# A new start order for a gated FFT and MLP mixer: dummy matmuls, block-wise hand-over, reordered vector work

## The chip, the cores and the metric

The kernel runs on one core of a Trainium2 chip. The metric is device time in microseconds (us) of that core for one launch. A run is called fast or slow by its state: slow means over 1.5% above the fastest run of the same kernel. Engines are called by their names in the profile: PE is the matmul engine, DVE the vector engine, ACT the scalar engine (activation functions, scaled copies), POOL the third elementwise engine, SP the engine whose queue issues most loads.

## The reference

Two branches read the same input x of S = 2048 rows and D = 512 columns and are mixed by a gate per row.

```python
x = A_x                                             # (1, 2048, 512) bf16
g = sigmoid((x * gate_w).sum(-1, keepdims=True))
# branch A: spectral mixing
a = irfft2(rfft2(x) * (w_r + 1j * w_i), s=(S, D))
# branch B: token MLP, along the rows; F = 1792
h = layernorm(x, axis=-1)
u = gelu(einsum("bsd,sf->bdf", h, w1) + b1)
b = (einsum("bdf,fs->bds", u, w2) + b2).transpose(0, 2, 1)
return g * a + (1 - g) * b
```

## The kernel before

Branch B is two matmul layers. The first one (`u`) has 14 groups of 16 matmuls; six groups use weights `w1a` and are accumulated side by side in six PSUM banks while the 16 row blocks of x come in, eight groups use weights `w1b` later. The second layer (`yb`) is 16 groups of 14 matmuls.

Branch A is a chain: DVE folds the transposed input into `xf`; PE does the transform along D (matmuls `f<-tf,xf`, called f1 below); ACT copies the result to `xdt`; DVE does a 16-point FFT (`pa` ... `fu`); PE does a second transform stage (`f<-fu,tce`, called f3); DVE multiplies by the spectral weights; then the way back: matmuls `i`, a second FFT on DVE (ending in `zt`), matmuls `ya`. PE fills its time between the steps of A with matmuls of B, in an order fixed when the kernel is built. In the first part the other engines are given their instructions in the order in which they are written. In the trace DVE keeps this order up to `xf`; the few instructions that stand behind `xf` in that part run mixed among those of the FFT.

The parts that the change touches (cuts marked):

```python
for b0, b1 in ((0, 2), (2, 6), (6, 11), (11, 16)):       # loads: x and its weights in turn
    w = wts.tile([P, b1 - b0, FT1 * P], BF16, tag="wt", name="w1a")
    nc.sync.dma_start(out=x[:, b0:b1], in_=xv[:, b0:b1])
    nc.sync.dma_start(out=w[:], in_=w1v[:, b0:b1, 0:FT1 * P])
# ... cut: bias loads; then xt (transposed x) and w1b loads; iotas in F32; tables tf
moments(0, 1)                       # mean and variance on DVE, 1/sqrt on POOL
# ... cut: index work for the tables
normal(0, 1, on_act=False)          # hn = (x - mean) * rstd, then six matmuls per block
moments(1, 3)
moments(3, 6)
normal(1, 3, on_act=False)
normal(3, 6)                        # from here on ACT writes hn
# ... cut: groups of three and four blocks, index work (fill_marg, tg) in between
nc.vector.tensor_add(marg3[:, 0], ea[:], m0[:, None, :].to_broadcast([P, NE, P]))
# ... cut: more index work, then prod = x * gate_w, then last of all:
for h in range(2):
    hs = slice(h * H, (h + 1) * H)
    nc.vector.tensor_add(xf[:, 0, :, hs], xt[:, 0:2, hs], xt[:, 2:4, hs])
    nc.vector.tensor_sub(xf[:, 1, :, hs], xt[:, 0:2, hs], xt[:, 2:4, hs])
# ... cut: gelus of the six groups, f1 with its copies, sine tables, gate sums
pw = a_bank("l0w")                  # a small reordering matmul, ahead of the FFT in the text
nc.tensor.matmul(pw[:, 0:64], lhsT=pmB[:], rhs=ws[:].rearrange("p e c w -> p (e c w)"),
                 start=True, stop=True)
# ... cut: arithmetic on its result
fft16(nc, tmp, xdt[:], fa[:], fu[:], inverse=False)
for e in range(NE):
    bank = a_bank("f3")
    nc.tensor.matmul(bank[:], lhsT=tce[:, 1, e, :], rhs=fu[:, e].rearrange("p c l -> p (c l)"),
                     start=True, stop=False)
    # ... cut
```

## Time and profile before

| | before |
|---|---|
| median of the first 4 runs (lowest to highest) | 156.96 us (156.03 to 157.4) |
| median of all 16 runs beside the result | 156.91 us (155.55 to 158.39) |
| span of the profiled run | 154.9 us |
| PE busy by the page | 136.2 us |
| PE work counted by matmul pitch | 124.7 us |

The pitch count is explained in the prediction below. It is needed since the recorded length of a matmul is not the time it takes from its neighbours: matmuls of 512 columns are recorded with a mean of 379 ns here, but follow each other every 216 ns. The Trainium skill, "Perfetto Trace Analysis", section "Tensor Engine Instruction (MATMUL, LD_WEIGHTS)", says that the end of a matmul is estimated by the profiler and is "a model, not a measurement"; this trace agrees.

From the page of the kernel before: the span, the busy times (us, share of the span, number of instructions), and the shares of engines in the chain of work that ended last.

```profile
span 154.9 us, 2013 instructions
...
PE 136.2 (88%) x697; PEld 68.1 (44%) x697; DVE 116.5 (75%) x279; ACT 94.7 (61%) x150; POOL 12.8 (8%) x37
...
DVE 58%; PE 21%; ACT 11%; issue 3%; DMA 3%; POOL 2%; POOLq 0%; ACTq 0%; DVEq 0%
```

The PE timeline of the kernel before from its start to the first matmuls with `w1b` (columns: start in us, length in us, engine, line, operation, out<-in, shapes, how many in a row, and in brackets the idle time before and what ended it):

```profile
6.85 0.18 PE L296 MATMUL bias_t<-ident,bias_rows 30*128 30x30 bf16 x1 [6.85 <-DVE ident L270]
7.34 2.72 PE L248 MATMUL u<-hn,w1a 128*128 128x512 bf16 x6 [0.31 <-DVE hn L245]
11.47 22.04 PE L248 MATMUL u<-hn,w1a 128*128 128x512 bf16 x90 [1.41 <-DVE hn L245]
34.55 1.67 PE L492 MATMUL u<-hn,w1b 128*128 128x512 bf16 x7 [1.03 <-ACT gl L334]
```

The first six matmuls take 2.72 us, about twice what six of them take later. As in the prediction, "first layer" means from here on the six groups with `w1a` alone, and "second-layer" matmuls those with `w1b`. The first layer begins at 7.34 us, and the first matmul with `w1b` stands at 34.55 us. This last number, "the start of `w1b`", is the mark for how long the first layer took.

All waits of PE in the kernel before (what waits, for what, us in total, times, longest):

```profile
PE bias_t L296 <- DVE ident L270: 6.8, 1, 6.8
PE l0w L379 <- DVE ws L377: 1.7, 1, 1.7
PE u L248 <- DVE hn L245: 1.7, 2, 1.4
PE ya L478 <- DVE zt L98: 1.2, 1, 1.2
PE ya L478 <- ACT eo L481: 1.1, 1, 1.1
PE u L492 <- ACT gl L334: 1.0, 1, 1.0
PE f L343 <- DVE xf L328: 0.3, 1, 0.3
```

The DVE timeline of the kernel before, around `xf` (same columns):

```profile
37.39 1.22 DVE L328 TENSOR_TENSOR xf<-xt 128x2048 bf16<-128x2048 bf16 x1
...
40.79 1.22 DVE L329 TENSOR_TENSOR xf<-xt 128x2048 bf16<-128x2048 bf16 x1
50.88 1.22 DVE L39 TENSOR_TENSOR pa<-xdt 128x2048 bf16<-128x2048 bf16 x1 [8.88 <-ACT xdt L345]
```

In the list of waits, the first line is only the start; the others are what the change may win. The last piece of `xf` ends at 42.0 us, 9 us after the last transposed input landed (32.94 us), and the FFT starts at 50.88 us.

The place of the wait for the small matmul, from the DVE and the PE timeline of the kernel before:

```profile
73.53 1.22 DVE L98 TENSOR_TENSOR fu<-pb,qb 128x2048 bf16<-128x2048 bf16 x1
78.45 0.41 PE L379 MATMUL l0w<-ws,pmB 128*128 128x64 f32 x2 [1.73 <-DVE ws L377]
```

The first piece of `fu` was ready at 74.75 us, 2 us before PE began to wait (76.72 us). f3 itself could have started then; only the small matmul, which stood ahead of it, could not.

One wait of this list is an accident of the profiled run, as its DVE timeline shows:

```profile
135.28 0.43 DVE L511 TENSOR_TENSOR ot<-tbv,ap 128x512 bf16<-128x512 bf16 x1 [1.27 <-DMA out_dram<-ot]
```

Here the second store of the output landed 3.89 us after its issue, while it takes 1.79 us in the profile of before_warm (below), which has the same instructions in this stage. The wait of 1.1 us for `eo` followed from it. So about 1.4 us of the profiled span of the kernel before are not there to be won by the change.

### The profile page before, as it was taken

To read this page: it belongs to the slowest core of one execution; us is meant where nothing else is said; L and a number is where in the kernel's file an instruction comes from. 1 tells how busy PE (TensorE), PEld (TensorE's weight loads), DVE (VectorE), ACT (ScalarE), POOL (GpSimd) and SP (SyncE) were. 2 spreads that over 40 slices of the span, in tenths; PEclk is the share of its full clock that TensorE was granted. 3 is DMA by queue.
4 is the path that set the end of the run, shared out by engine and by line. 5 is a ranking of instruction groups with operands and counts; after the bars stand their busy time and mean duration, and the time that the engine had idled before them with its cause. 6 is when DMAs were issued, how large, how long until landed. Compare 5 with 4: busy or idle time off the path is not lost.

```text
span 154.9 us, 2013 instructions
## 1 busy us (share of the span) xinstructions
PE 136.2 (88%) x697; PEld 68.1 (44%) x697; DVE 116.5 (75%) x279; ACT 94.7 (61%) x150; POOL 12.8 (8%) x37
## 2 busy tenths in 40 slices
PE   0169999979999999999879999999999969969990
PEld 0023444433555544444345564465444435645430
DVE  3998979969800499999986999508999999598111
ACT  3305764997199999999529895475232244778221
POOL 7127625000000000000000000000000000000000
PEclk9999999999999999999999999999999999999997
DMA  4999999999999006180700700430348000424210
GB/s 145 353 383 389 244 205 297 200 280 347 340 292 320 15 0 181 56 235 14 225 0 28 213 2 0 129 108 4 99 138 236 1 0 0 140 102 142 92 37 34
DMA packets 41816, 23.33 MB, mean 151 GB/s; under 512 B 9008, under 2 KB 41776, under 8 KB 41808
## 3 DMA queue, kind: packets, MB, share of 16 engines
q1 hardware_dynamic: 41696, 23.08, 52.1%
q0 software_dynamic: 112, 0.14, 0.4%
q8 instruction: 5, 0.08, 0.2%
q14 instruction: 3, 0.02, 0.1%
HBM read 19.02 MB, written 2.10 MB: 136 GB/s over the span
## 4 chain that ended last, share of the span: by engine, by line
DVE 58%; PE 21%; ACT 11%; issue 3%; DMA 3%; POOL 2%; POOLq 0%; ACTq 0%; DVEq 0%
PE yb L505 9%; DVE stats L230 6%; PE f L343 5%; DVE ta L407 3%; DVE tb L408 3%; DMA out_dram<-ot 3%; ACT tice L204 2%; DVE prod L323 2%; ACT tce L204 2%; ACT hn L242 2%; DVE marg L258 2%; DVE y L409 2%; PE ya L478 2%; DVE pb L39 2%; POOL rstd L234 2%
## 5 line engine op out<-in xcount | busy, mean ns | idle before, releaser
L505 PE MATMUL yb<-gl,w2t 128*128 128x512 bf16 x224 | 53.6, 379 | 0.0
L505 PEld LDWEIGHTS <-w2t 128*128 128x128 bf16 x224 | 21.9, 98 | 21.4 <-issue 0.2
L492 PE MATMUL u<-hn,w1b 128*128 128x512 bf16 x128 | 29.3, 379 | 1.0 <-ACT gl L334 1.0
L507 ACT ACTIVATE tbv<-yb,ombb,omg 128x512 bf16<-128x512 f32 x16 | 12.4, 777 | 23.8 <-PE yb L505 22.4
L248 PE MATMUL u<-hn,w1a 128*128 128x512 bf16 x96 | 24.8, 425 | 1.7 <-DVE hn L245 1.7
L492 PEld LDWEIGHTS <-w1b 128*128 128x128 bf16 x128 | 12.5, 98 | 14.9 <-issue 1.3
L248 PEld LDWEIGHTS <-w1a 128*128 128x128 bf16 x96 | 10.2, 106 | 16.0 <-issue 7.1
L242 ACT ACTIVATE hn<-x,nmr,rstd 128x512 bf16<-128x512 bf16 x13 | 9.6, 802 | 9.2 <-DVE nmr L239 7.1
L481 ACT ACTIVATE eo<-ya,gs 128x512 bf16<-128x512 f32 x16 | 10.5, 687 | 5.6 <-DVE ap L484 3.5
L511 DVE TENSOR_TENSOR ot<-tbv,ap 128x512 bf16<-128x512 bf16 x16 | 6.6, 420 | 8.8 <-ACT tbv L507 7.5
L345 ACT CAST xdt<-f 128x512 bf16<-128x512 f32 x16 | 10.7, 734 | 3.7 <-DVE xf L329 3.2
L418 ACT CAST xs<-f 128x512 bf16<-128x512 f32 x16 | 9.1, 587 | 4.1 <-PE f L417 3.8
L478 PE MATMUL ya<-tg,zt 128*128 128x256 bf16 x64 | 9.3, 271 | 2.5 <-DVE zt L98 1.2
L466 ACT CAST vp<-i 128x512 bf16<-128x512 f32 x16 | 8.8, 586 | 2.8 <-PE i L464 2.6
L352 ACT ACTIVATE junk<-prod 128x512 bf16<-128x512 bf16 x16 | 10.0, 626 | 0.3
L230 DVE BATCH_NORM_STATS2 stats<-x 128x6 f32<-128x512 bf16 x16 | 10.1, 680 | 0.0
L343 PE MATMUL f<-tf,xf 128*128 128x256 bf16 x64 | 9.6, 271 | 0.4 <-DVE xf L328 0.3
L334 ACT ACTIVATE gl<-u,biases 128x512 bf16<-128x512 f32 x14 | 9.0, 684 | 0.8 <-PE u L492 0.8
L478 PEld LDWEIGHTS <-zt 128*128 128x128 bf16 x64 | 6.1, 97 | 6.7 <-issue 2.7
L343 PEld LDWEIGHTS <-xf 128*128 128x128 bf16 x64 | 6.0, 96 | 5.2 <-issue 3.2
L462 PE MATMUL i<-tice,y 128*128 128x256 bf16 x32 | 7.8, 272 | 0.1
L39 DVE TENSOR_TENSOR pa<-xdt 128x2048 bf16<-128x2048 bf16 x1 | 1.2, 1224 | 8.9 <-ACT xdt L345 8.9
(178 smaller groups left out, 182.7 us busy)
## 6 DMA issues: line engine op xcount, KB each, us to landing
w2t<-in_B_w_dram SPq DMA_DIRECT2D x8, 896.0 KB, 4.9
w1b<-in_B_w_dram SPq DMA_DIRECT2D x4, 1024.0 KB, 7.2
out_dram<-ot SPq DMA_DIRECT2D x16, 128.0 KB, 1.7
w1a<-in_B_w_dram SPq DMA_DIRECT2D x2, 960.0 KB, 10.7
x<-in_A_x_dram SPq DMA_DIRECT2D x2, 640.0 KB, 9.6
wri<-in_A_w_r_dram SPq DMA_DIRECT2D x1, 1028.0 KB, 9.6
wri<-in_A_w_i_dram SPq DMA_DIRECT2D x1, 1028.0 KB, 10.2
w1a<-in_B_w_dram SPq DMA_DIRECT2D x1, 768.0 KB, 6.9
```

The source lines that it names most:

```text
L230: nc.vector.bn_stats(out=stats[:, b, :], in_=x[:, b, :])
L242: nc.scalar.activation(hn[:, b, :], x[:, b, :], ActF.Identity, bias=nmr[:, b:b + 1], scale=rstd[:, b:b + 1])
L248: nc.tensor.matmul(u1[ft][:], lhsT=w1a[b][:, ft * P:(ft + 1) * P], rhs=hn[:, b, :], start=(b == 0), stop=(b == NB - 1))
L343: nc.tensor.matmul(bank[:, par * L:(par + 1) * L], lhsT=xf[:, par, kt, b * P:(b + 1) * P], rhs=tf[:, kt, par], start=(kt == 0), stop=(kt = ...
L345: nc.scalar.copy(xdt[:, b].rearrange("p c (i t) -> p t c i", t=2), bank[:].rearrange("p (t c i) -> p t c i", t=2, c=2))
L352: nc.scalar.activation(junk[:], prod[:, b], ActF.Copy, accum_out=glog[:, b:b + 1])
L418: nc.scalar.copy(xs[:, e], bank[:].rearrange("p (c l) -> p c l", c=2))
L478: nc.tensor.matmul(bank[:, par * L:(par + 1) * L], lhsT=zt[:, b, comp, par, :], rhs=tg[:, par, comp, :], start=(comp == 0), stop=(comp == 1))
L481: nc.scalar.activation(eo[:], bank[:].rearrange("p (t d) -> p t d", t=2), ActF.Copy, scale=gs[:, b:b + 1])
L492: nc.tensor.matmul(u[:], lhsT=w[:, b, k * P:(k + 1) * P], rhs=hn[:, b, :], start=(b == 0), stop=(b == NB - 1))
L505: nc.tensor.matmul(yb[:], lhsT=w[:, ft, k * P:(k + 1) * P], rhs=gl[:, ft, :], start=(ft == 0), stop=(ft == NFT - 1))
L507: nc.scalar.activation(tbv[:, b, :], yb[:], ActF.Identity, bias=ombb2[:, b:b + 1], scale=omg[:, b:b + 1])
```

## The change

The intent is to have PE do useful work, at full clock, from as early as possible, and to bring the vector chain forward by the same amount:

1. Twelve dummy matmuls on zeros at the very start, so that the clock is up when real ones come.
2. The first load of x split into one block and one block; two iotas ahead of the bias loads; index tables in 16 bits.
3. Layer norm handed over block by block (DVE for blocks 0 to 4), then in pairs (ACT).
4. The tables' index work moved behind `xf`; `xf` made in halves of the inputs that land first. The product with the gate weights in place.
5. The gelu table loaded ahead of its first use; two groups of the second weights ("early") issued ahead of f1.
6. The small reordering matmul moved from ahead of f3 into its loop; negated tables and gate scales behind the forward FFT. DVE now keeps the written order to the end of branch A.

The core of the diff (cuts marked by `...`):

```diff
+    zero = tmp.tile([P, D], BF16, tag="tws", name="zero")
+    nc.vector.memset(zero[:], 0.0)
+    warm = a_bank("warm")
+    for _ in range(WARM):                        # WARM = 12
+        nc.tensor.matmul(warm[:], lhsT=zero[:, 0:P], rhs=zero[:], start=True, stop=True)
...
-    for b0, b1 in ((0, 2), (2, 6), (6, 11), (11, 16)):
+    groups = {0: 2, 2: 6, 6: 11, 11: 16}
+    for b0, b1 in ((0, 1), (1, 2), (2, 6), (6, 11), (11, 16)):
...
-    m1t = tmp.tile([P, 2, 2, 2 * P], I32, tag="ffp", name="m1t")
+    m1t = tmp.tile([P, 2, 2, 2 * P], U16, tag="ffp", name="m1t")
...
+    moments(0, 1)
+    for b in range(1, 5):
+        moments(b, b + 1)
+        normal(b - 1)                            # hn on DVE
+    moments(5, 6)
+    normal(4)
+    moments(6, 8)
+    normal_act(5, 6)                             # hn on ACT
+    moments(8, 10)
+    normal_act(6, 8)
...
-        nc.vector.tensor_mul(prod[:, bs], x[:, bs], gwb[:, None, :].to_broadcast([P, 4, D]))
+        nc.vector.tensor_mul(x[:, bs], x[:, bs], gwb[:, None, :].to_broadcast([P, 4, D]))
+    nc.scalar.activation(pre[:], c_mhalf, ActF.Gelu_apprx_tanh)
...
-    for h in range(2):
-        hs = slice(h * H, (h + 1) * H)
-        nc.vector.tensor_add(xf[:, 0, :, hs], xt[:, 0:2, hs], xt[:, 2:4, hs])
-        nc.vector.tensor_sub(xf[:, 1, :, hs], xt[:, 0:2, hs], xt[:, 2:4, hs])
+    for k in range(2):
+        nc.vector.tensor_add(xf[:, 0, k], xt[:, k], xt[:, k + 2])
+        nc.vector.tensor_sub(xf[:, 1, k], xt[:, k], xt[:, k + 2])
...
+    gate_sum(0, 6)
+    for k in range(2):                           # two early groups with w1b
+        u = mm_bank("u2")
+        for b in range(NB):
+            nc.tensor.matmul(u[:], lhsT=w1b[k // 2][:, b, k % 2 * P:(k % 2 + 1) * P], rhs=hn[:, b, :], ...)
...
+    for e in range(NE):                          # index work, now behind xf
+        nc.vector.tensor_scalar_add(marg[:, 0, e], m0[:], ae[:, e:e + 1])
+    nc.vector.tensor_scalar_add(marg[:, 1], marg[:, 0], 1536.0)
+    mask(marg, 2048)
...
+    fft16(nc, tmp, xdt[:], fa[:], fu[:], inverse=False)
+    nc.vector.tensor_scalar_mul(tce[:, 2], tce[:, 0], -1.0)
+    nc.vector.tensor_scalar_mul(tice[:, :, 2], tice[:, :, 0], -1.0)
...
-    pw = a_bank("l0w")                           # ahead of the f3 loop
...
+        if e == 7:                               # inside the f3 loop
+            packed_weights()
```

## The prediction

> **What bounds it now.** By the page's busy shares PE (the matmul engine) is busy 136.2 of the 154.9 us span. Counting each matmul at its steady start-to-start pitch in the PE timeline (512 columns 216 ns, 256 columns 108 ns), PE's work is 124.7 us; it runs from 6.9 to 150.7 us, so it loses about 19 us between, plus 6.9 us before and 4.2 us after (last scaling, add, store). The vector engine's chain (58% of the chain of waits) does not bind at the end: its ya stage ends near 141 us and 44 dense yb matmuls follow. So I cost the change as PE time.
>
> **Where PE loses time (PE timeline):**
> - 23 of the 96 first-layer matmuls run at a pitch of 427 ns until 16.5 us, then 216: about 4.9 us. The Trainium skill, "TensorE: Matmul & The Clock Gate", Part 1, says the array runs at half clock until busy for about one window of 3.4 us; the trace agrees (2.7 us of work, a hole, then 5 us more before the switch).
> - Waiting for normalised input, 10.0 to 11.5 us: 1.4.
> - Waiting for a bank at the first gelu, behind a 1.28 us table load: 1.2.
> - Waiting for the small reordering matmul's data before the second spectral stage: 1.7.
> - Before and in the last stage, for zt and eo: 2.3. The rest is unevenness in interleaved stages.
>
> **What the change does.**
> 1. Twelve dummy matmuls from about 1 us: at 427 ns each up to 5 us, while PE waits anyway. The clock should be full for nearly all real matmuls.
> 2. First row block loaded alone, index work in 16 bits, iota before the bias loads: first real matmul at about 5.3 us, not 7.3.
> 3. But weights of blocks 2 to 5 land at 9.2 us and inputs of blocks 6 to 10 at 11.0 us (landings of DMAs); the queue is full, so this hardly moves. I expect short waits there; the first layer ends at about 28.3 us instead of 33.4 (saves 5, not the 7 that points 1 and 2 promise).
> 4. Gelu table preloaded: 0.5 us. Small matmul moved into the spectral stage: 1.7 us.
> 5. xf in halves, cosine-table work moved behind xf. The last transposed input landed at 32.9 us, so xf ends near 35.5 instead of 42; evacuation (16 x 0.70 us) ends near 47.5; the forward FFT near 70; the second spectral stage starts near 70.5 instead of 78.9. The vector chain is about 8 us earlier: it keeps up with PE, but yields no more than PE saves.
> 6. In-place products and fused gate sums: off the path.
>
> **Sum.** PE saves 5 + 0.5 + 1.7, and perhaps 2.5 of the remaining waits: about 9.7 us. The tail stays 4.2 us. Predicted 147.2 us, range 143.5 to 151.0. Chances: faster 0.93, same 0.06, slower 0.01.
>
> **What would show the steps.** First real matmul near 5.3 us, pitch 216 ns from about 6 us; first layer ends 27.5 to 29; PE holes near 8-9 and 13-15 us; no wait on the reordering matmul; xf ends near 35.5; second spectral stage starts 69 to 72; the span still ends in dense yb matmuls (15 to 40).
>
> **What would make it wrong.** PE's order is fixed by a scheduler: early second-layer matmuls hold two banks until their gelus; if those queue behind the sine tables and gate sums, PE could stall several us near 55. If the vector chain ends behind PE, the gain shrinks. If holes cool the clock again, the start gives back up to 3 us.

## The result and the profile after

The kernel after took 150.5 us (median of 11 runs, 149.76 to 151.38) beside 156.91 us (16 runs) for the kernel before. The ratio is 0.9612, with a 95% interval of 0.9576 to 0.9649. Here and below a ratio is the mean time of one kernel's fast runs over the mean of the other's fast runs of the same rounds, so it is not quite the ratio of the medians. The profiled run of the kernel after took 149.39 us, less than any of the other eleven; this matters below.

From the page of the kernel after (same three parts):

```profile
span 147.5 us, 2055 instructions
...
PE 137.1 (93%) x709; PEld 68.9 (47%) x709; DVE 118.6 (80%) x289; ACT 92.6 (63%) x149; POOL 14.5 (10%) x42
...
PE 42%; DVE 18%; SPq 16%; ACT 15%; DMA 4%; issue 2%; DVEq 0%; ACTq 0%
```

PE's busy time hardly moved, while the span shrank. Of the chain, 42% now runs through PE, after 21% before.

The PE timeline of the kernel after, up to f1:

```profile
1.20 4.68 PE L153 MATMUL warm<-zero 128*128 128x512 bf16 x12 [1.20 <-DVE zero L150]
6.47 6.96 PE L244 MATMUL u<-hn,w1a 128*128 128x512 bf16 x30 [0.59 <-DVE hn L248]
14.49 1.46 PE L244 MATMUL u<-hn,w1a 128*128 128x512 bf16 x6 [1.06 <-ACT hn L256]
16.17 2.75 PE L244 MATMUL u<-hn,w1a 128*128 128x512 bf16 x12 [0.22 <-ACT hn L256]
...
18.97 10.53 PE L244 MATMUL u<-hn,w1a 128*128 128x512 bf16 x48
29.34 7.07 PE L345 MATMUL u<-hn,w1b 128*128 128x512 bf16 x32
36.25 1.04 PE L352 MATMUL f<-tf,xf 128*128 128x256 bf16 x8
```

The start of `w1b` moved from 34.55 to 29.34 us: 5.2 us. The whole span shrank by 7.4 us (7.3 before rounding). So 5.2 of the 7.4 us come from the first layer with the hole behind it, and 2.2 us from everything that follows, of which about 1.4 us are the late store of the profile before.

All waits of PE in the kernel after:

```profile
PE f L440 <- ACT gl L335: 1.5, 1, 1.5
PE u L244 <- ACT hn L256: 1.3, 2, 1.1
PE warm L153 <- DVE zero L150: 1.2, 1, 1.2
PE ya L506 <- DVE zt L100: 1.1, 1, 1.1
PE u L244 <- DVE hn L248: 0.6, 1, 0.6
```

Compare the two lists after the first layer. The wait for the small matmul (1.7) is gone, but a wait of 1.5 stands at the first f3 matmul (`f<-fu,tce`, line 440), at nearly the same place in the program. The wait for `zt` stayed (1.2 and 1.1). The wait for `eo` (1.1), which came from the late store, and the bubble at the first gelu (1.0) went. In the kernel before the gelu stood behind a table load of 1.28 us; the Trainium skill, "ScalarE: Activation LUTs", "What ACT_TABLE_LOAD costs", gives about 1283 ns for one, and the trace agrees.

The name "ACT gl" in the first line is misleading. Here is DVE's instruction that makes the first piece of `fu`, from the DVE timeline of the kernel after:

```profile
66.21 1.22 DVE L100 TENSOR_TENSOR fu<-pb,qb 128x2048 bf16<-128x2048 bf16 x1
```

And here is the waiting matmul, from the PE timeline of the same kernel:

```profile
67.57 0.59 PE L440 MATMUL f<-fu,tce 128*128 128x512 bf16 x2 [1.49 <-ACT gl L335]
```

`fu` is ready at 67.43 us and the gelu happened to end within 0.03 us of it (67.46 us), so the profile put the wait down to the gelu. An experiment below decides between the two.

The DVE timeline of the kernel after, around `xf`:

```profile
32.78 1.22 DVE L331 TENSOR_TENSOR xf<-xt 128x2048 bf16<-128x2048 bf16 x1
...
45.49 1.23 DVE L41 TENSOR_TENSOR pa<-xdt 128x2048 bf16<-128x2048 bf16 x1 [2.85 <-ACT xdt L354]
```

`xf` is done at 34.0 us instead of 42.0, the FFT starts 5.4 us earlier, and its first output comes 7.3 us earlier.

Finally, what starts the first layer. The DVE timeline of the kernel after from 5 us:

```profile
4.99 0.69 DVE L236 BATCH_NORM_STATS2 stats<-x 128x6 f32<-128x512 bf16 x1 [0.96 <-DMA x<-in_A_x_dram]
...
6.01 0.40 DVE L248 TENSOR_SCALAR hn<-x,mv,rstd 128x512 bf16<-128x512 bf16 x1
6.51 0.69 DVE L236 BATCH_NORM_STATS2 stats<-x 128x6 f32<-128x512 bf16 x1
...
7.85 0.69 DVE L236 BATCH_NORM_STATS2 stats<-x 128x6 f32<-128x512 bf16 x1
```

Two things are to be seen. DVE took the statistics of block 1 first and had to wait for its load (landed 4.97 us); only then did it write `hn` of block 0. And block 2, whose load landed at 6.49 us, was started at 6.51 us. From there DVE needs 1.33 us per block (6.51 to 7.85 us), while six matmuls at 216 ns need 1.30 us: PE can't run ahead of DVE.

### The profile page after: what moved, and what is told of

Read it like the earlier page. It is cut to its first block, busy times and chain, and to the rows that moved or that the text cites. A ratio compares the mean times of both kernels' runs of the same rounds, so it can differ in the third digit from the quotient of the medians.

```text
span 147.5 us, 2055 instructions
## 1 busy us (share of the span) xinstructions
PE 137.1 (93%) x709; PEld 68.9 (47%) x709; DVE 118.6 (80%) x289; ACT 92.6 (63%) x149; POOL 14.5 (10%) x42
## 4 chain that ended last, share of the span: by engine, by line
PE 42%; DVE 18%; SPq 16%; ACT 15%; DMA 4%; issue 2%; DVEq 0%; ACTq 0%
PE yb L538 19%; SPq L180 11%; PE ya L506 6%; PE f L352 5%; ACT x L312 4%; DMA xt<-in_A_x_dram 4%; SPq L165 3%; PE f L440 3%; PE i L490 3%; ACT tce L210 3%; ACT tice L210 2%; ACT gl L335 2%; PE i L492 2%; SPq L161 2%; DVE idx L360 2%
## 5 line engine op out<-in xcount | busy, mean ns | idle before, releaser
L538 PE MATMUL yb<-gl,w2t 128*128 128x512 bf16 x224 | 54.4, 379 | 0.0
L244 PE MATMUL u<-hn,w1a 128*128 128x512 bf16 x96 | 21.6, 379 | 1.9 <-ACT hn L256 1.3
L525 PE MATMUL u<-hn,w1b 128*128 128x512 bf16 x96 | 22.2, 379 | 0.0
L256 ACT ACTIVATE hn<-x,nmr,rstd 128x512 bf16<-128x512 bf16 x11 | 8.3, 805 | 11.9 <-DVE nmr L254 11.8
L244 PEld LDWEIGHTS <-w1a 128*128 128x128 bf16 x96 | 9.3, 97 | 13.8 <-issue 3.4
L525 PEld LDWEIGHTS <-w1b 128*128 128x128 bf16 x96 | 9.4, 97 | 10.3
L312 ACT ACTIVATE x<-x 128x512 bf16<-128x512 bf16 x16 | 9.8, 630 | 0.0
L240 POOL TENSOR_TENSOR rstd<-rstd,consts 128x1 f32<-128x1 f32 (+1 forms) x11 | 7.3, 664 | 11.2 <-DVE rstd L239 5.7
```

Source lines behind the costliest of these rows:

```text
L244: nc.tensor.matmul(u1[ft][:], lhsT=w1a[b][:, ft * P:(ft + 1) * P], rhs=hn[:, b, :], start=(b == 0), stop=(b == NB - 1))
L312: nc.scalar.activation(x[:, b], x[:, b], ActF.Copy, accum_out=glog[:, b:b + 1])
L525: nc.tensor.matmul(u[:], lhsT=w[:, b, k * P:(k + 1) * P], rhs=hn[:, b, :], start=(b == 0), stop=(b == NB - 1))
L538: nc.tensor.matmul(yb[:], lhsT=w[:, ft, k * P:(k + 1) * P], rhs=gl[:, ft, :], start=(ft == 0), stop=(ft == NFT - 1))
```

## The experiments

Theories in short. For the start: the clock theory says that cold matmuls cost the time and the dummies win it back; the supply theory says that loads and normalisation set the pace, and the dummies buy nothing. For what follows: the wait at f3 comes from gelus held up behind gate sums (as the profile names it), or from the FFT on DVE. And for the vector order: it is slack that only keeps up, or a condition of the gain. Twelve kernels ran. A first build of the twelfth deadlocked in the simulator and never ran on a chip.

The result table first (ratio to the kernel before of the same rounds). The medians are of all runs; three of the six of before_xf_first and two of the six of after_fine were slow, and the ratios leave these out:

| run | median us (lowest to highest) | ratio, 95% interval |
|---|---|---|
| before_warm | 156.33 (155.24 to 156.83) | 0.9988, 0.9939 to 1.0036 |
| after_cold | 151.11 (150.35 to 152.16) | 0.9661, 0.9613 to 0.9709 |
| after_few_sums | 150.57 (149.76 to 151.6) | 0.963, 0.9572 to 0.9688 |
| after_small_first | 152.44 (152.02 to 153.03) | 0.9757, 0.9712 to 0.9801 |
| after_fine | 150.74 (149.31 to 151.97) | 0.9594, 0.9544 to 0.9644 |
| after_bias | 150.45 (149.58 to 150.75) | 0.9608, 0.9575 to 0.964 |
| after_tables_first | 155.78 (155.28 to 157.43) | 0.9976, 0.9924 to 1.0028 |
| before_xf_first | 159.05 (156.72 to 160.19) | 1.0065, 0.9995 to 1.0134 |
| after_hold | 149.98 (149.79 to 150.56) | 0.9596, 0.9562 to 0.963 |
| after_hold2 | 148.44 (147.65 to 149.19) | 0.9477, 0.9428 to 0.9525 |
| best | 148.75 (148.29 to 149.82) | 0.9505, 0.9459 to 0.9551 |
| after_hold3 | 147.75 (147.44 to 148.84) | 0.9466, 0.9419 to 0.9514 |

### The dummies alone, on the kernel before (before_warm)

```diff
+    zero = tmp.tile([P, D], BF16, tag="ffs", name="zero")
+    nc.vector.memset(zero[:], 0.0)
+    warm = a_bank("warm")
+    for _ in range(12):
+        nc.tensor.matmul(warm[:], lhsT=zero[:, 0:P], rhs=zero[:], start=True, stop=True)
```

> The kernel before with only the twelve dummy matmuls added. Theory (supply): the dummies remove the slow clock (first-layer matmuls at a pitch of 216 instead of 427 ns), but the PE then waits for hn, which comes at 11.4, about 13, 18.6, 22 and 26.4 us as before; the first layer ends near 30.0 us instead of 33.5, and the time falls by 3.0 to 3.8 us (153 to 154). Rival (bookkeeping of the prediction): the whole 4.9 us of slow clock is saved, 152.0 us. Second rival: the clock falls back in the waits and under 1.5 us is saved.

It took 156.33 us, the same as the kernel before (155.91 us in these rounds). Both theories with a large saving fell; the second rival held. The windows of this run show what the clock did (columns: window in us and its length, then busy us and number of instructions of PE, weight loads, DVE, ACT, POOL, then the granted clock, the DMA share and GB/s):

```profile
5.54:8.95 3.41, 2.17 (x10) 0.81 (x9) 3.19 (x14) 0.98 (x2) 0.60 (x1) 1.00 1.06 382
8.95:12.36 3.41, 0.89 (x5) 0.41 (x5) 2.95 (x11) 0.00 (x1) 1.89 (x4) 1.00 1.07 393
12.36:15.78 3.42, 3.42 (x10) 1.19 (x9) 3.38 (x12) 2.22 (x3) 2.43 (x10) 0.50 1.07 395
```

The clock was up at 5.54 us. In the second window PE was busy for only 0.89 of 3.41 us, since it waited 2.68 us for the second block of `hn`, and in the third the clock was at half. The matmuls ran sooner, so they ran out of input sooner, and the wait brought the cold clock back. The start of `w1b` came at 34.15 us instead of 34.55.

The cold clock is not the whole story, though. One of the six runs, of 155.95 us, lists a mean granted clock of 0.999, which leaves no room for such a window, and it gained nothing either. The ACT timeline of the profiled run shows a second bound:

```profile
28.40 3.69 ACT L210 ACTIVATE tce<-marg,consts 128x4096 bf16<-128x4096 int16 x1
32.12 1.28 ACT L340 ACT_TABLE_LOAD   x1
```

ACT was busy with the cosine table `tce` until 32.09 us, and the table load and the first gelu, which frees the first bank for `w1b`, followed without a pause. A faster first layer alone could not have started `w1b` much earlier. In the kernel after, the gelu table is loaded by 26.83 us and `tce` comes later.

### The kernel after without the dummies (after_cold)

```diff
-    warm = a_bank("warm")
-    for _ in range(WARM):
-        nc.tensor.matmul(warm[:], lhsT=zero[:, 0:P], rhs=zero[:], start=True, stop=True)
```

> The changed kernel without its dummy matmuls. Theory (supply): the first 10 to 16 first-layer matmuls run at 427 ns, the PE falls behind by 2 to 3 us, but the waits for hn at 13.1 to 14.5 and at 15.8 to 16.2 us take most of it up; the first layer ends 0.3 to 1.5 us later than in the changed kernel and the time rises by as much. Rival (bookkeeping): the 4.9 us of slow clock comes back, at least 3.5 us slower.

The median is 151.11 us, against 150.57 for after_few_sums, whose PE order and vector order at the start are those of the kernel after. The clock rose at 10.99 us, so the matmuls of the first 4.6 us ran at half clock. And yet the start of `w1b` came at 29.87 us, only 0.5 us later than in the profile of the kernel after, and all of this is a later landing of one load, as the following table shows. The dummies thus bought next to nothing at this mark: for the kernel after, the supply theory is right.

That table puts together all profiled runs whose start is that of the kernel after. The load is that of x blocks 2 to 5.

```
run                  load landed   start of w1b   difference
after                   6.49          29.34         22.85
after_few_sums          6.58          29.43         22.85
after_cold              7.01          29.87         22.86
after_hold3             7.30          30.15         22.85
after_tables_first      7.40          30.25         22.85
after_hold2             7.51          30.36         22.85
after_bias              7.52          30.36         22.84
after_hold              8.08          30.93         22.85
after_small_first       8.46          31.32         22.86
```

The first layer begins with one load and then takes 22.85 us, with the dummies and without them. The landing differs between runs of the same load instructions by 2 us. It is the largest part of what differs between profiles of like kernels, so below I also quote the span minus this landing: 141.0 us for the kernel after and 141.1 for after_few_sums, 141.5 for after_cold.

### The bias loads from another queue (after_bias)

The suspicion was that the small bias loads from POOL's queue push the x load back.

```diff
-    nc.gpsimd.dma_start(out=bias_rows[0:NFT], in_=B_b1.rearrange("(ft f) -> ft f", f=P))
+    nc.scalar.dma_start(out=bias_rows[0:NFT], in_=B_b1.rearrange("(ft f) -> ft f", f=P))
```

> The changed kernel with its two small bias loads issued from ACT a little later, in place of POOL at 1.4 and 2.1 us. In one trace the load of blocks 2 to 5 of x landed at 6.5 us, in another at 8.5 us, with the transfer rate down while the bias packets ran. Theory (these packets disturb): it lands near 6.0 us in the trace, the runs spread less (highest minus lowest under 1.0 us, against 1.6) and the median falls by 0.3 to 0.9 us. Rival: the dip has another cause; no change, spread the same.

It took 150.45 us, no different from the kernel after, and its load landed at 7.52 us. So another queue doesn't help. But ACT issued the two loads at 2.83 and 4.64 us, when the x load was still under way, so they aren't cleared as the cause. What makes the landing move between 6.5 and 8.5 us stays open.

### The first layer in single blocks throughout (after_fine)

```diff
-    moments(6, 8)
-    normal_act(5, 6)
-    moments(8, 10)
-    normal_act(6, 8)
+    for b in range(6, 10):
+        moments(b, b + 1)
+        normal_act(b - 1, b)
```

(The later pairs were changed in the same way, and one iota was moved up.)

> The changed kernel with the normalisation of blocks 5 to 15 handed over one block at a time instead of two, and the small index ramp that the identity needs made at the start (the vector engine waited 0.87 us for it). Theory: the two waits for hn (1.23 and 0.39 us beyond the pitch, at 13.1 and 15.6 us) mostly go, the first layer ends near 28.2 us instead of 29.5, and all of it reaches the end: 1.0 to 1.6 us faster than the changed kernel. Rival: later waits in the fixed PE order swallow it, under 0.4 us.

There was no clear gain: 150.74 us, with two of six runs slow, the profiled one among them. In that profile the start of `w1b` came 22.33 us after the load, so 0.5 us was won, and then PE stood still for want of weights (PE timeline):

```profile
39.77 0.61 PE L523 MATMUL u<-hn,w1b 128*128 128x512 bf16 x2 [1.49 <-DMA w1b<-in_B_w_dram]
```

In this run the second tile of `w1b` landed too late for a faster first layer, at 39.72 us; in the profile of the kernel after it landed at 36.60 us.

### The small matmul back ahead of f3 (after_small_first)

```diff
+    packed_weights()
     for e in range(NE):
...
-        if e == 7:
-            packed_weights()
```

> The changed kernel with the small reordering matmul put back ahead of the second spectral stage. Theory: moving it saved nothing by itself, as the PE's order, fixed before the run, puts something that needs the forward FFT there in both cases; the wait of 1.5 us at the first matmul of the spectral stage goes and one of 1.5 to 2.2 us for the reordering matmul's data comes; time within 0.7 us of the changed kernel. Rival (prediction, point 4): it is 1.7 us slower than the changed kernel.

It took 152.44 us, 1.9 us more than the kernel after and than after_few_sums of the same rounds (150.57 us). The two ratios lie apart, so by the runs the move is worth what the prediction gave to it, and the theory's "within 0.7 us" failed. The profile shows less. Its x load landed at 8.46 us, 1.97 us later than in the profile of the kernel after. The span minus landing is 141.7 us, against 141.1 for after_few_sums: about 0.6 us for the move, an estimate from one profile each. The wait for the small matmul's input came back, and that for `fu` went (PE timeline):

```profile
75.04 0.41 PE L412 MATMUL l0w<-ws,pmB 128*128 128x64 f32 x2 [1.99 <-DVE ws L407]
```

It isn't that one wait hid the other. The first piece of `fu` was ready at 69.42 us here, and PE worked until 73.05 us. What changed is the order: with the small matmul ahead of f3, 20 `yb` matmuls stand before f3 in this trace, and none in that of the kernel after. So in the kernel after f3 came too early for the FFT, and here it stood behind a small matmul that came too early for its own input.

What separates 0.6 from 1.9 us is open. The profiled run was the fastest of the six, and lists a mean clock of 0.996; the other five list 0.984 to 0.989. A loss of 0.01 over 150 us is about 3 us at half clock (an estimate), so these runs probably had one more cold window than the profiled one. None of them has a trace.

### Half of the gate sums (after_few_sums; result wrong on purpose)

```diff
-    gate_sum(6, NB)
+    gate_sum(6, 8)
+    nc.vector.memset(glog[:, 8:NB], 0.0)
```

> The changed kernel with only 8 of the 16 gate sums on ACT (the result is wrong on purpose). It asks who holds the PE at 66.1 to 67.6 us, where the profile names ACT's gelu. Theory: the forward FFT on DVE; the wait stays at 1.3 to 1.7 us although the gelus come about 5 us earlier, and the time changes by less than 0.5 us. Rival (the risk the prediction named): gelus queue behind the gate sums; the wait goes and the time falls by about 1.5 us.

The time stayed (150.57 us), and so did the wait at f3, although ACT had half of the sums to do. The PE timeline of this run:

```profile
67.66 0.59 PE L441 MATMUL f<-fu,tce 128*128 128x512 bf16 x2 [1.49 <-DVE fu L100]
```

The gelus now came sooner, and the profile names the true releaser: the FFT on DVE. The outputs were off by a relative error of 0.0228, as intended.

### The index work back ahead of xf (after_tables_first)

```diff
+    for e in range(NE):
+        nc.vector.tensor_scalar_add(marg[:, 0, e], m0[:], ae[:, e:e + 1])
+    # ... the same lines for marg and marg3, taken from behind xf
     xf = plane([P, 2, 2, S], "xf")
```

> The changed kernel with the vector engine's cosine-table index work (about 7.7 us) back ahead of xf. Theory A (as the prediction has it, the earlier vector chain is only slack): at most 0.8 us slower. Theory B: the PE has no other work at 36.2 us, as the second tile of weights lands at 36.6 us and its fixed order has the f matmuls next; it waits about 4 us for xf there, and the time rises by 3 to 5 us.

It took 155.78 us: the whole gain was gone (ratio 0.9976). The PE timeline of this run:

```profile
39.20 0.39 PE L359 MATMUL f<-tf,xf 128*128 128x256 bf16 x2 [1.88 <-DVE xf L337]
41.47 0.61 PE L359 MATMUL f<-tf,xf 128*128 128x256 bf16 x4 [1.88 <-DVE xf L337]
```

PE had finished the first layer early and run out of other work, and then waited twice for `xf`. The waits also brought the clock down for the next window (same columns as above):

```profile
38.79:42.20 3.41, 1.12 (x8) 0.68 (x9) 3.41 (x4) 0.00 (x0) 0.00 (x0) 1.00 1.15 345
42.20:45.61 3.41, 3.41 (x13) 1.64 (x12) 1.24 (x6) 1.32 (x2) 0.00 (x0) 0.50 1.20 306
```

### The reverse: xf first in the kernel before (before_xf_first)

The `xf` block of the kernel before was moved ahead of the index work for the second table and of the gate products, nothing else.

```diff
+    xf = plane([P, 2, 2, S], "xf")               # moved up, unchanged
+    for h in range(2):
+        ...
     marg3 = tmp.tile([P, 2, NE, P], I16, tag="ffr", name="marg3")
```

> The kernel before with only its xf block moved ahead of the second table's index work and the products, so that it waits for nothing but the transposed input (landed 32.9 us): xf ready for the first f matmuls near 35.3 us instead of 38.6, the last part near 37.5 instead of 42. Theory (the PE bounds the kernel before and hardly waits for xf there, 0.45 us): time within 1.2 us of the kernel before, either way. Rival (the vector chain binds the kernel before): the forward FFT starts 4 to 5 us earlier and the time falls by 3 us or more.

It was no faster: the ratio of the fast runs is 1.0065. Three of its six runs, the profiled one among them, were slow, so its profile may only be used for order. It shows PE waiting for `xf` all the same:

```profile
35.30 0.61 PE L343 MATMUL f<-tf,xf 128*128 128x256 bf16 x2 [3.43 <-DVE xf L317]
```

The scheduler now placed f1 directly behind the first layer, where the last transposed input had only just landed, and there were no early groups to fill the hole. So in these two kernels the early `xf` was worth nothing without the new start, and the new start was worth nothing without the early `xf`. Since the order of PE changed too, the first half is not shown for the early `xf` as such.

### Holding f3 and ya back (after_hold, after_hold2, best, after_hold3)

PE's matmuls run in the order in which they are laid down. In the kernel after, the first f3 matmul waits for `fu`, and the first ya matmul for `zt`, while matmuls that are ready stand behind them. The Trainium skill, "TensorE: Matmul & The Clock Gate", Part 2, "Step-by-step: what each phase is for", says that only weight loads are pulled ahead and "the MATMULs themselves stay in program order"; all traces here agree, as the wait of 1.49 us in the kernel after shows, behind which two ready `u` matmuls stood. after_hold changes the order alone: it lays 23 `yb` matmuls ahead of the first f3 matmul, and more ahead of the first ya matmul, by two ordering edges without a semaphore.

```diff
+                for n, late in ((HOLD_F3, f3_first), (HOLD_YA, ya_first)):     # 22 and 162
+                    if b * NFT + ft == n:
+                        tc.add_manual_dep(late.ins, yb_in.ins.name, ...)       # order only
```

> The changed kernel with two added ordering edges alone: the first matmul of the second spectral stage is put behind 23 yb matmuls in the PE's order, the first ya matmul behind at least 163. No instruction is added or removed. Theory (the PE's order, fixed before the run, sends it to these two places too early): the waits of 1.66 and 1.27 us beyond the pitch go, and the time falls by 2.2 to 2.9 us. Rival (the vector chain binds there): the PE's work is only brought forward, other waits open in the spectral or the last stage, and under 0.7 us is saved.

The wait for `fu` was gone, but the time fell by only about 0.5 us (149.98). ACT had received the finished `yb` groups earlier, and its timeline shows what that did:

```profile
74.15 0.78 ACT L550 ACTIVATE tbv<-yb,ombb,omg 128x512 bf16<-128x512 f32 x1 [4.52 <-DVE ombb L403]
```

ACT stood still for 4.52 us until this scaling had its gate scale, which DVE makes behind the FFT. The copies `xs` of f3's results stood behind it in ACT's order, so that PE waited 1.19 us for them. The wait at ya (1.09 us in this run's PE timeline) stayed too.

after_hold2 takes both lessons: it holds f3 behind 13 `yb` matmuls only, makes the gate scales right behind the first output of the FFT, and puts the negated tables in the middle of it.

```diff
-HOLD_F3 = 22
+HOLD_F3 = 12
...
-    nc.vector.tensor_scalar_mul(tce[:, 2], tce[:, 0], -1.0)      # behind the FFT
+    fft16(nc, tmp, xdt[:], fa[:], fu[:], inverse=False, mid=negatives, late=gate_scales)
```

> The changed kernel with ordering edges that hold the first spectral-stage matmul behind 13 yb matmuls and the first ya matmul behind so many that 98 instead of 91 yb matmuls stand between the last inverse-stage matmul and it; and, since in the first try ACT's evacuation of yb waited for ombb (74.0 us) ahead of the xs casts, the negated tables are made in the middle of the forward FFT and omg, gs, ombb behind its first output. Theory (order and in-order queues, not supply): the waits of 1.66 and 1.27 us beyond the pitch fall under 0.5 each with no new one over 0.6, and the time falls by 1.8 to 2.8 us against the changed kernel (ratio to the kernel before near 0.945). Rival (the vector chain binds): the waits move elsewhere, ratio 0.955 or more.

It took 148.44 us, 2.1 us less than the kernel after by the medians, with ratios to the kernel before of 0.9477 against 0.9612 and intervals that don't touch. In its PE timeline no wait is left at f3:

```profile
67.38 2.97 PE L552 MATMUL yb<-gl,w2t 128*128 128x512 bf16 x13
70.19 0.38 PE L450 MATMUL f<-fu,tce 128*128 128x512 bf16 x1
```

The wait at the first ya matmul had moved on: the third pair of ya groups now waited 1.29 us for ACT's copies. The run called best adds after_fine to after_hold2, and lays three matmuls with `w1b` between pairs of f1.

```diff
+                if n % 3 == 2 and n < 18:
+                    tc.add_manual_dep(f1_first[2 * (n // 3) + 4].ins, u_in.ins.name, ...)
```

> The edges and moves of the run before, the one-block-at-a-time normalisation, and edges that put three second-layer matmuls instead of one between pairs of f banks from the third pair on (there the PE waits 0.43 us a pair for ACT's casts). Theory: the f stage loses about 1 us less, the first layer about 0.5, so 0.5 to 1.5 us faster than the run before. Rival: the second weight tile, which lands at 36.6 us or later, binds the f stage; no further gain.

It took 148.75 us, no better than after_hold2: it waited for the second tile of `w1b` again (0.98 us by the PE timeline), and 1.25 us for `fu`. after_hold3 instead adds one edge to after_hold2, which lays about ten `yb` matmuls ahead of the third pair of ya groups.

```diff
+HOLD_YA2 = 174
...
+                for n, late in ((HOLD_F3, f3_first), (HOLD_YA, ya_first[0]), (HOLD_YA2, ya_first[4])):
```

> The second held kernel with one more edge: the third pair of ya banks behind about ten yb matmuls instead of three. In the run before, the edge at the first ya bank only moved the wait of 1.3 to 1.45 us there to that third pair, since it used up the yb matmuls that stood there while ACT waited for the vector engine's ap. Theory (the PE's order): that wait falls under 0.6 us and the time falls by another 0.8 to 1.5 us, to a ratio near 0.938. Rival: the last stage is bound by ACT and the vector engine one after the other, and the wait moves on again: within 0.4 us of the run before.

It took 147.75 us, the least of all, with a ratio of 0.9466 to the kernel before. It beats both kernels; from after_hold2 it is not separated, since their intervals overlap. The wait at the third pair did go (two of 0.3 us or less remain for `eo`), but the ratio moved by 0.001 only, so the theory's gain of 0.8 us or more is not shown.

## Why the prediction was right or wrong

The predicted time was 147.2 us with a range of 143.5 to 151.0, and 150.5 us lies inside it, near the upper end. The direction and most of the size were right; some terms of the sum were not. The prediction's sum is 9.7 us. The profiled spans differ by 7.4 us, and the median of the kernel after is 1.1 us above its profiled run (150.5 and 149.39 us).

- "The first layer ends at about 28.3 us instead of 33.4": it ended at 29.3 us, where `w1b` begins, so it saved 4.0 us and not 5. "Gelu table preloaded: 0.5 us" was sized too small in turn: the hole of 1.2 us ahead of `w1b`, from 33.35 to 34.55 us, closed wholly. Together 5.5 us were predicted and 5.2 us measured. The cause was not the first one on the prediction's list: "run at a pitch of 427 ns until 16.5 us, then 216: about 4.9 us" counted the cold clock as a loss that dummies can win back. The count was too high as well: in the trace 18 matmuls, not 23, start before 16.48 us, a loss of 3.8 us. before_warm won 0.4 us at that mark, and after_cold showed that the same 22.85 us pass after the load with a cold clock. What won the time is the supply of normalised blocks. An estimate from the trace of the kernel before says how much the clock could have done there: at 216 ns per matmul, with every `hn` as it came, the first layer would have ended at about 31.7 us, against 33.35 measured and 29.34 in the kernel after. That ACT no longer makes the cosine table (3.69 us) ahead of the first gelu was needed for it too; this is argued from ACT's timelines. Which part of the new start (split load, iotas, 16-bit tables, hand-over by blocks) brought how much was not tested. What the prediction says of the clock itself was right: it starts at half pitch (427 and 216 ns), as the Trainium skill, "TensorE: Matmul & The Clock Gate", Part 1, has it, and "if holes cool the clock again, the start gives back up to 3 us" is what happened in before_warm, though not in the kernel after.
- "First real matmul near 5.3 us": it came at 6.47 us. The step overlooked that DVE takes the statistics of block 1, and waits for its load, before it writes `hn` of block 0. Of the two expected holes "near 8-9 and 13-15 us" only the second came (1.06 us, up to 14.49 us).
- "Small matmul moved into the spectral stage: 1.7 us": a wait of 1.73 us went and one of 1.49 us came in at the first f3 matmul, so the two wait lists give 0.2 us, and the profile of after_small_first about 0.6 us. The step left out that the order of PE is made anew: 149 matmuls with `w1b` and of `yb` stood before f3 in the trace of the kernel before, and 126 in that of the kernel after, so f3 met the forward FFT before it was ready. after_few_sums showed that DVE, and not the gelus, sets this wait, and after_hold2 that another order takes it away. By the runs of after_small_first the term is 1.9 us; whether the rest comes from the clock stays open.
- "Perhaps 2.5 of the remaining waits" (a guess without a named wait): 7.4 less 5.2 and 0.2 leaves about 2.0 us, but about 1.4 us of this is the late store in the profile before, a matter of luck. So the change won some 0.6 us here. The wait for `zt` stayed.
- "xf ends near 35.5", "the forward FFT near 70", "second spectral stage starts 69 to 72": `xf` ended at 34.0, the FFT's last output at about 71, and f3 began at 67.57, since it needs only the first output. "It keeps up with PE, but yields no more than PE saves" holds as it stands: before_xf_first won nothing by it. But the sum gave it no part, and after_tables_first shows that without it the gain is nil. It was a condition of every other term.
- "PE could stall several us near 55", behind early matmuls that wait for their gelus: this risk did not come true. The wait list has nothing between the first layer and f3.
- "The span still ends in dense yb matmuls (15 to 40)": it did, with 44, as before, a little more than the range.

With these, 147.2 becomes 147.2 + 1.0 (first layer) - 0.7 (gelu) + 1.5 (small matmul) + 0.5 (other waits) = 149.5 us, which is the profiled run (149.39). That it fits proves nothing, since the last term was taken as what remained. The remaining 1.1 us up to the median is most likely the landing of the x load, for in the profiled run it landed earlier than in any other profile of these kernels. This is argued from the table of landings, not shown: the other eleven runs have no trace.

The lists of runs hint at one more part of the gain that neither the prediction nor the profiles have. Of the 44 runs of the kernel before in the four rounds of experiments, 23 list a mean clock of 0.983 to 0.989 and have a median of 157.0 us, and 21 list 0.993 or more and have 155.8 us. All twelve runs of the kernel after list 0.993 or more. So the kernel before probably falls to half clock for one window in about every second run (an estimate as above), and the kernel after does not. No such run of it was traced, so where this happens is open; in the slow profile of before_xf_first such a window follows on the wait for the small matmul, at 78.59 us.

## What to carry to other kernels

Before you count a cold clock or a wait as a saving, ask what would be waited for next: find the load or the engine that supplies PE, and compare its pace per block (1.33 us here) with PE's (1.30 us). When two engines are close to being the limit, cost their changes together: without the early `xf` the new start won nothing here, the early `xf` without the new start won nothing either, and the whole change won 6 us. And look for an accident of the one profiled run, such as a late load or store, before you count its waits. And when matmuls have a fixed order, a wait with ready work behind it can be taken away by order alone, if the engine that takes over the results is not then held up itself.

## What the Trainium skill lacked or had wrong

- "TensorE: Matmul & The Clock Gate", Part 1 (table of the states) and "Why this matters for your kernels": the page has the clock fall after an idle window of about 3.4 us and warns of idle gaps above about 3 us. Here it fell with shorter gaps: in before_warm after one gap of 2.68 us, and in after_tables_first after two gaps of 1.88 us with matmuls in between. What fits these runs is the busy share of one window of 3.41 us: the clock fell at 0.89 and 1.12 us busy, and did not fall at 1.95 us (after_tables_first, the window before) or 1.99 us (after_small_first). By this count the limit lies near 1.6 us: the clock held at 1.61 us in the kernel after (141.66 to 145.07 us) and fell at 1.62 us in the slow profile of before_xf_first (75.17 to 78.59 us). The busy time uses the recorded lengths of matmuls, so it is rough. The length of the window agrees with the page (all records of the clock that begin and end inside a run are multiples of 3.413 us).
- The same part: the page has the clock rise after a busy window of about 3.4 us. In the kernel before it did not rise after windows with 2.49 and 2.00 us busy (counted back from the rise in steps of 3.413 us), and rose only after a full one, at 16.48 us. In after_bias it rose at 4.29 us after a window with 3.10 us busy. So less than a full window was enough to rise, and more was needed to rise (over 2.49 us) than to stay up (1.61 us). How busy a window must be is not on the page.
- No page has the spread of a load's landing between runs: the same load of 512 KB, issued at about 2.2 us each time, landed between 6.49 and 8.46 us in the nine profiles of the table, and the kernel's time followed it.
